# Sorting the late queue of a backward kernel by chunk: chunk 0's operations unpinned, chunk 1's put off by one iteration

## The chip, the core and the metric

The kernel runs on one core of a Trainium2 chip. The metric is the device time of one execution in microseconds (us); lower is better. A core has five engines that run side by side and meet through semaphores: TensorE (PE, matmuls), VectorE (DVE), ScalarE (ACT), GpSimd (POOL) and SyncE (SP, which here only issues DMAs). Each engine takes its instructions in a fixed order.

## The reference: what is computed

Forward pass and all gradients of a speech joint network. Two convolutions over time (3 taps, each followed by gelu and by taking every second step) reduce 16000 steps to 4000; the result is projected, combined with 8 label vectors by tanh, and projected again.

```python
def _fwd_reference(x, w1, w2, g, w_f, w_g, w_o):
    ...
    xp = jnp.pad(x, ((0,0),(pad,pad),(0,0)))
    h = jnp.zeros_like(x)
    for i in range(K):
        h = h + jnp.einsum("btc,cd->btd", xp[:, i:i+T, :], w1[i])
    h = _gelu(h)[:, ::2, :]
    ...
    f = _gelu(f)[:, ::2, :]
    fe = jnp.einsum("btd,de->bte", f, w_f)
    ge = jnp.einsum("bud,de->bue", g, w_g)
    j = jnp.tanh(fe[:, :, None, :] + ge[:, None, :, :])
    return jnp.einsum("btud,dv->btuv", j, w_o)

def reference(x, w1, w2, g, w_f, w_g, w_o, grad_out):
    ...
    _out, _vjp = jax.vjp(_f, x, w1, w2, g, w_f, w_g, w_o)
    _grads = _vjp(grad_out)
```

x is 2 x 16000 x 256 in bf16, the output 2 x 4000 x 8 x 256. For each gelu the kernel needs its value in the forward pass and its derivative in the backward pass.

## The kernel before

The 4000 steps of each of the two batches are cut into 8 chunks of 512 (CW, the last one 416): 16 chunks, numbered n. A loop over n (line 783) does in iteration n: the joint part of chunk n (tanh, output, gradients, in four steps "up" of two labels u each), the backward convolutions of chunk n - 1, and the forward convolutions of chunk n + 1. The forward part of chunk 0 is done ahead of the loop (the prologue, line 777), so iteration 0 has the forward part of chunk 1 and no backward part.

The units of work are Python generators. `weave` (line 702) steps through the joint part (`joint_units`) and takes, by a ratio, units of a `fill` chain, which holds the convolutions. After each joint unit it calls `pump`, which emits operations of two queues: `later`, the first half of a gelu (its value), and, when that is empty, `lazy`, the second half (its derivative).

`gelu` (line 202) makes both halves. The first has a square on ACT (g_sq), a step on DVE (line 214, g_s), a sigmoid on ACT (g_s again) and a product on DVE, which gives HT or FT. The second has five DVE operations on the same scratch tiles: two tensor_scalar and three tensor_tensor, which give the derivative G1 or G2. All the emitted calls of the first half stand at line 198 or 291 in the profile, those of the second at line 200. A chunk has three gelus (even and odd steps of the first convolution, and the second convolution), so 15 operations of 128 x 1024; chunk 0 does each in two halves of 128 x 512, so 30. The scratch tiles come from a pool of three buffers per name (`gel3`); chunk 0 takes tiles of `rows` (pool `rowp`, six) instead. With a chunk's second halves two small copies on POOL go into the queue: G1h, the last column of G1 kept for the next chunk, and G, that column's place in the next chunk.

A scheduler decides the order of the instructions on each engine when the program is built. What is wrapped in `tc.keep_in_program_order` ("pinned") stays where the program emits it; other instructions may be moved ahead or back, as their data allow. In the kernel before, `pump` pins every operation of `lazy`:

```python
            elif lazy and lazy_on[0]:
                tc.keep_in_program_order(lazy.popleft()())
```

`lazy_on` is set when the second convolution of the next chunk has been emitted (line 295), and cleared at the end of each iteration, after the whole queue has been emptied (lines 832 and 833). The flag is first set in the prologue, by chunk 0. So in iteration 0 the 30 operations of chunk 0 and the 15 of chunk 1 are all emitted; in a later iteration n, the 15 of chunk n + 1. They are first read in iteration n + 2: G2 by line 354 (GF), G1 by line 385 (GH).

Other lines that matter: 249 (first convolution, PE) and 252 (its eviction, ACT, g_x); 283 and 286 (second convolution, the same); 306 and 308 (FE, the projection); 316 (tanh, JT); 540 (JSQ, the square of JT, ACT); 546 (gradient of JT, PE, with weights WOT and the loaded GOT) and 548 (its product with 1 - JT squared, DVE, NGZ); 567 (sum of NGZ over u, POOL, ACCN); 396 and 398 (JT transposed on PE and copied to JR by DVE in iteration 0; later iterations do it with a DMA, line 580); 644 and 646 (output block, PE, and its eviction OUT, ACT); 693 (gradient of w_o, PE, GWO_ps); 333 and 335 (the other weight gradients' accumulation, DVE, ACC). PSUM has seven tiles for all of these results ("ps" and "pst", pool `psp`).

Of the kernel before, what the change touches and what calls it, by code (L numbers as in the profile page):

```python
# [28 lines left out]
CW = 512  # L29
# [4 lines left out]
def kernel(  # L34
# [22 lines left out]
    nc = tc.nc  # L57
# [7 lines left out]
    def geom(n):  # L65
        b, ci = chunks[n]
        c0 = ci * CW
        return b, ci, c0, min(CW, MQ - c0)
# [33 lines left out]
    def ps_f32():  # L102
        return psp.tile([P, 512], FP32, name="ps", tag="ps")
# [24 lines left out]
    S = [dict() for _ in range(G)]  # L128
# [61 lines left out]


    later, lazy = deque(), deque()
    lazy_on = [False]

    def pump(k):
        for _ in range(k):
            if later:
                later.popleft()()  # L198
            elif lazy and lazy_on[0]:
                tc.keep_in_program_order(lazy.popleft()())  # L200

    def gelu(xb, W, h, gp, off, kts=((0, KT),), spare=False, pinned=False):

        pin = tc.keep_in_program_order if pinned else (lambda ins: ins)
        sq, s = scratch("g_sq", spare), scratch("g_s", spare)
        TT, TS, STT = nc.vector.tensor_tensor, nc.vector.tensor_scalar, nc.vector.scalar_tensor_tensor
        first, second = [], []
        for (k0, k1) in kts:
            sq_, s_, x_ = sq[:, k0:k1, :W], s[:, k0:k1, :W], xb[:, k0:k1, :W]
            h_, gp_ = h[:, k0:k1, off:off + W], gp[:, k0:k1, off:off + W]  # L210
            first += [
                partial(nc.scalar.activation, out=sq_, in_=x_, func=ACT.Square, scale=ROOT_K),
                lambda s_=s_, sq_=sq_, x_=x_: pin(
                    STT(out=s_, in0=sq_, scalar=1.0, in1=x_, op0=ALU.add, op1=ALU.mult)),  # L214
                partial(nc.scalar.activation, out=s_, in_=s_, func=ACT.Sigmoid, scale=GELU_A),
                partial(TT, out=h_, in0=s_, in1=x_, op=ALU.mult),
            ]
            second += [
                partial(TS, out=sq_, in0=sq_, scalar1=3.0 * GELU_A, scalar2=GELU_A, op0=ALU.mult, op1=ALU.add),
                partial(TS, out=gp_, in0=s_, scalar1=-1.0, scalar2=1.0, op0=ALU.mult, op1=ALU.add),  # L220
                partial(TT, out=sq_, in0=sq_, in1=gp_, op=ALU.mult),
                partial(TT, out=sq_, in0=sq_, in1=h_, op=ALU.mult),
                partial(TT, out=gp_, in0=sq_, in1=s_, op=ALU.add),
            ]
        return first, second
# [4 lines left out]
    def conv_units(n):  # L230
        b, ci, c0, W = geom(n)
        seconds = []
        st = S[n]
        HT = htp.tile([P, 2, KT, CW + 2], BF16, name="HT")
        G1 = g1p.tile([P, 2, KT, CW + 2], BF16, name="G1")
        st["HT"], st["G1"] = HT, G1
        if ci == 0:
            nc.gpsimd.memset(HT[:, 1, :, 1:2], 0.0)
        else:
            nc.gpsimd.tensor_copy(out=HT[:, 1, :, 1:2], in_=S[n - 1]["HT"][:, 1, :, CW + 1:CW + 2])  # L240
        taps = {0: ((1, 0, 0), (2, 1, 0), (0, 3, -1)), 1: ((0, 1, 0), (2, 3, 0), (1, 2, 0))}
        for par in range(2):
            xb = gel.tile([P, KT, CW], BF16, name="g_x")
            for mt in range(KT):
                ps = ps_f32()
                k = 0
                for (i, c, sh) in taps[par]:
                    for kt in range(KT):
                        nc.tensor.matmul(ps[:, :W], lhsT=W1[:, i, kt, mt * P:(mt + 1) * P],  # L249
                                         rhs=st["X", c][:, kt, 16 + sh:16 + sh + W], start=(k == 0), stop=(k == 5))  # L250
                        k += 1
                nc.scalar.copy(out=xb[:, mt, :W], in_=ps[:, :W])
                yield
            first, second = gelu(xb, W, HT[:, par], G1[:, par], 2, HALVES if n == 0 else ((0, KT),), n == 0,
                                 pinned=n > 1 and par == 1)
            later.extend(first)
            seconds += second
            if n == 0:
                pump(len(first))
        lazy.extend(seconds)  # L260
        if ci > 0:
            lazy.append(lambda: nc.gpsimd.tensor_copy(out=G1[:, :, :, 1:2], in_=S[n - 1]["G1h"][:]))
        if ci < NCH - 1:
            st["G1h"] = halo.tile([P, 2, KT, 1], BF16, name="G1h")
            lazy.append(
                lambda: nc.gpsimd.tensor_copy(out=st["G1h"][:], in_=G1[:, :, :, CW + 1:CW + 2]))

    def conv2_units(n):
        b, ci, c0, W = geom(n)
        st = S[n]  # L270
        HT = st["HT"]
        if n > 0:
            pump(len(later))
        FT = ftp.tile([P, KT, CW], BF16, name="FT")
        G2 = ftp.tile([P, KT, CW], BF16, name="G2")
        st["FT"], st["G2"] = FT, G2
        xb = gel.tile([P, KT, CW], BF16, name="g_x")
        for mt in range(KT):
            ps = ps_f32()
            k = 0  # L280
            for (i, par, off) in ((1, 0, 2), (0, 1, 1), (2, 1, 2)):
                for kt in range(KT):
                    nc.tensor.matmul(ps[:, :W], lhsT=W2[:, i, kt, mt * P:(mt + 1) * P],  # L283
                                     rhs=HT[:, par, kt, off:off + W], start=(k == 0), stop=(k == 5))
                    k += 1
            nc.scalar.copy(out=xb[:, mt, :W], in_=ps[:, :W])
            yield
        first, second = gelu(xb, W, FT, G2, 0, HALVES if n == 0 else ((0, KT),), n == 0)
        if n == 0:
            for f in first:  # L290
                f()
        else:
            later.extend(first)
        lazy.extend(second)
        lazy_on[0] = True

    def fe_units(n):
        b, ci, c0, W = geom(n)
# [484 lines left out]
    for n in range(G):  # L783
        back, fwd = n > 0, n + 1 < G
        conv = conv_units(n + 1) if fwd else iter(())
        parts = []
        if back:
            for (o, M) in blocks(window(n - 1)[1] - window(n - 1)[0]):
                load_x5(n - 1, o, M)
            d1, e, gwf = d1_units(n - 1), e_units(n - 1), gwf_units(n - 1)  # L790
            nfn = (len(blocks(geom(n - 1)[3])) + 1) // 2
            d5, gw2 = d5_units(n - 1), gw2_units(n - 1)
            nhg = KQ
            parts += [islice(conv, 2), islice(d1, 1), islice(conv, 1), d1, islice(conv, 1),
                      islice(gwf, 1), islice(d5, 1), conv, islice(gwf, nfn - 1), islice(d5, 1), islice(gw2, 1),
                      islice(d5, 1), islice(gw2, 1), d5, islice(gw2, nhg - 2), gwf, gw2]
        else:
            parts += [conv, iter([None] * 3)]
        conv2 = conv2_units(n + 1) if fwd else iter(())
        if back:  # L800
            parts += [islice(e, 1), islice(conv2, 1), islice(e, 1), conv2, islice(e, 5)]
        else:
            parts.append(conv2)
            parts.append(iter([None] * 3))
        if fwd:
            parts.append(fe_units(n + 1))
        if back:
            parts.append(e)
        fill = chain(*parts)
        ratio = (0.85 if n > 0 else 0.28) if n + 1 < G else 0.72  # L810
        for up in range(U // 2):
            step = n * (U // 2) + up
            if n + 2 < G:
                load_x(n + 2, (1, 0, 3, 2)[up])
            if step + 1 < len(orderp):
                load_go(*orderp[step + 1])
            for i in range(2):
                if 2 * step + 4 + i < len(order):
                    load_got(*order[2 * step + 4 + i])

            def ahead():
                for i in range(2):
                    if 2 * step + 2 + i < len(order):
                        tanh(*order[2 * step + 2 + i])
                if step + 1 < len(orderp):
                    load_jr(*orderp[step + 1])

            weave(joint_units(n, up, ahead), fill, ratio)
            if up == U // 2 - 1:
                for _ in fill:  # L830
                    pump(2)
                pump(len(later) + len(lazy))
                lazy_on[0] = False
    def small_gradients():
        t_ = gel.tile([P, 512], BF16, name="g_x", tag="g_x")
        nc.scalar.copy(out=t_[:], in_=GWO_ps[:].rearrange("p k v -> p (k v)"))
# [32 lines left out]
    n = G - 1  # L869
# [35 lines left out]
```

## Time and profile before

| | us |
|---|---|
| median of 3 runs | 854.25 (853.19 to 855.17) |
| the profiled execution | 852.57, its span 850.8 |
| PE busy | 821.0 (96%) |
| ACT busy | 680.5 (80%) |
| DVE busy | 628.5 (74%) |
| POOL busy | 392.1 (46%) |

The mean granted TensorE clock of the profiled execution is 0.992. The costliest groups of instructions of the DVE and POOL are these (line, engine, operation, out<-in, shapes, count; busy us, mean ns of one; idle time before them and what ended most of it):

```profile
L567 POOL TENSOR_TENSOR ACCN<-ACCN,NGZ 128x1024 f32<-128x1024 f32 (+1 forms) x80 | 168.4, 2104 | 126.2 <-DVE NGZ L548 124.2
...
L548 DVE SCALAR_TENSOR_TENSOR NGZ<-JSQ,ps 128x512 bf16<-128x512 bf16 (+1 forms) x256 | 166.0, 668 | 26.9 <-PE ps L546 21.6
...
L214 DVE SCALAR_TENSOR_TENSOR g_s<-g_sq,g_x 128x1024 bf16<-128x1024 bf16 (+1 forms) x45 | 58.1, 1291 | 67.9 <-ACT g_sq L198 67.5
```

A stage is read with the busy time of each engine in a stretch of the span; a wait of an engine is put down to the instruction that released it.

### The profile page before, as it was taken

What the parts mean: (1) busy time and instruction counts of PE and PEld (TensorE: products, weight loads), DVE (VectorE), ACT (ScalarE), POOL (GpSimd) and SP (SyncE); (2) the same over time, 40 slices, a digit from 0 to 9 for tenths busy, and PEclk for the clock granted to TensorE, in tenths of its full rate; (3) what the DMA queues carried; (4) which work ended last, traced back from release to release, by engine and by line L of the source; (5) the groups of instructions that cost most, each with busy time, mean ns of one, the idle gap of its engine ahead of it and who ended that gap; (6) DMA issues with size and microseconds to landing.
All of it is one profiled execution on the core that took longest, in us unless ns stands there. A gap on an engine that the chain in (4) does not pass through costs nothing.

```text
span 850.8 us, 17235 instructions
## 1 busy us (share of the span) xinstructions
PE 821.0 (96%) x6478; PEld 600.5 (71%) x6552; DVE 628.5 (74%) x1190; ACT 680.5 (80%) x1064; POOL 392.1 (46%) x452
## 2 busy tenths in 40 slices
PE   8877999999999999999999999999999999999998
PEld 4444776777767677787767678677777767777876
DVE  4599777687877868777776887767797776868552
ACT  4786989697997969798796969969797896979533
POOL 1144454454444445454554644444553544545650
PEclk9998999999999999999999999999999999999999
DMA  9976999999999999999999999999999999998942
GB/s 187 188 156 148 232 234 187 227 238 203 238 259 215 239 233 235 247 213 243 205 261 210 247 218 244 172 223 267 219 252 204 247 285 201 251 242 193 226 146 90
DMA packets 379280, 185.60 MB, mean 218 GB/s; under 512 B 326786, under 2 KB 362907, under 8 KB 379198
## 3 DMA queue, kind: packets, MB, share of 16 engines
q1 hardware_dynamic: 359550, 115.19, 75.9%
q0 software_dynamic: 19648, 69.32, 26.0%
q8 instruction: 51, 0.84, 0.4%
q14 instruction: 31, 0.25, 0.1%
HBM read 54.43 MB, written 50.34 MB: 123 GB/s over the span
## 4 chain that ended last, share of the span: by engine, by line
PE 56%; ACT 21%; DVE 16%; issue 4%; DMA 2%; POOL 0%; SPq 0%; DVEq 0%; ACTq 0%; POOLq 0%
PE ps L644 8%; PE GWO_ps L693 7%; PE ps L546 7%; ACT JT L316 7%; PE ps L495 7%; PE ps L518 6%; PE ps L454 5%; DVE NGZ L548 5%; PE ps L283 4%; PE pst L396 4%; ACT OUT L646 3%; PE ps L249 3%; ACT JSQ L540 3%; DVE G L200 3%; DVE HT L198 3%
## 5 line engine op out<-in xcount | busy, mean ns | idle before, releaser
L567 POOL TENSOR_TENSOR ACCN<-ACCN,NGZ 128x1024 f32<-128x1024 f32 (+1 forms) x80 | 168.4, 2104 | 126.2 <-DVE NGZ L548 124.2
L540 ACT ACTIVATE JSQ<-JT 128x1024 bf16<-128x1024 bf16 (+1 forms) x128 | 133.2, 1046 | 73.4 <-DVE NGZ L548 72.4
L548 DVE SCALAR_TENSOR_TENSOR NGZ<-JSQ,ps 128x512 bf16<-128x512 bf16 (+1 forms) x256 | 166.0, 668 | 26.9 <-PE ps L546 21.6
L316 ACT ACTIVATE JT<-FE,GE 128x512 bf16<-128x512 f32 (+1 forms) x256 | 170.2, 721 | 0.5
L646 ACT CAST OUT<-ps 128x512 bf16<-128x512 f32 x248 | 145.4, 599 | 16.8 <-PE ps L644 16.7
L644 PE MATMUL ps<-WO,JT 128*128 128x256 bf16 x992 | 149.3, 275 | 9.1 <-DVE NGZ L548 6.2
L546 PE MATMUL ps<-GOT,WOT 128*128 128x512 bf16 (+1 forms) x472 | 135.6, 376 | 5.7 <-DVE JR L398 3.0
L693 PE MATMUL GWO_ps<-GO,JR 128*128 128x256 bf16 x992 | 140.8, 275 | 0.0
L644 PEld LDWEIGHTS <-JT 128*128 128x128 bf16 x992 | 96.0, 98 | 37.9 <-issue 11.0
L693 PEld LDWEIGHTS <-JR 128*128 128x128 bf16 x992 | 95.9, 99 | 18.9 <-issue 1.6
L214 DVE SCALAR_TENSOR_TENSOR g_s<-g_sq,g_x 128x1024 bf16<-128x1024 bf16 (+1 forms) x45 | 58.1, 1291 | 67.9 <-ACT g_sq L198 67.5
L673 POOL DMA_DIRECT2D out_dram<-OUT x64 | 49.6, 774 | 119.1 <-ACT OUT L646 117.2
L495 PE MATMUL ps<-W1T,GH 128*128 128x256 bf16 (+2 forms) x768 | 104.2, 273 | 0.0
L498 ACT CAST GX<-ps 128x512 bf16<-128x512 f32 (+2 forms) x128 | 74.8, 584 | 23.8 <-PE ps L495 19.1
L249 PE MATMUL ps<-XC,W 128*128 128x512 bf16 (+1 forms) x370 | 88.9, 375 | 3.8 <-DMA XC<-in_x_dram 3.4
L518 PE MATMUL ps<-rows,X 128*128 128x256 bf16 (+2 forms) x768 | 92.3, 273 | 0.0
L495 PEld LDWEIGHTS <-GH 128*128 128x128 bf16 (+2 forms) x768 | 75.0, 99 | 12.4 <-issue 0.8
L518 PEld LDWEIGHTS <-X 128*128 128x128 bf16 (+2 forms) x768 | 74.6, 98 | 12.9 <-issue 1.3
L546 PEld LDWEIGHTS <-WOT 128*128 128x128 bf16 x512 | 49.0, 98 | 45.8 <-issue 5.7
L335 DVE TENSOR_TENSOR ACC<-ACC,ps 128x512 f32<-128x512 f32 x84 | 57.3, 682 | 28.8 <-PE ps L454 24.2
L249 PEld LDWEIGHTS <-W 128*128 128x128 bf16 x384 | 37.7, 98 | 41.2 <-issue 4.5
L508 POOL DMA_DIRECT2D out_dram<-GX x60 | 33.7, 561 | 71.9 <-ACT GX L498 67.9
(138 smaller groups left out, 1309.0 us busy)
## 6 DMA issues: line engine op xcount, KB each, us to landing
GO<-in_grad_out_dram SPq DMA_DIRECT2D x56, 512.0 KB, 5.2
out_dram<-OUT POOLq DMA_DIRECT2D x56, 512.0 KB, 5.8
X<-in_x_dram POOLq DMA_DIRECT2D x58, 320.0 KB, 8.6
out_dram<-GX POOLq DMA_DIRECT2D x55, 256.0 KB, 4.9
GO<-in_grad_out_dram SPq DMA_DIRECT2D x8, 384.0 KB, 3.8
out_dram<-OUT POOLq DMA_DIRECT2D x8, 384.0 KB, 4.8
JR<-JT SPq DMA_TRANSPOSE x136, 5.9
GOT<-in_grad_out_dram SPq DMA_TRANSPOSE x128, 5.2
```

The costliest lines, as they stand in the source:

```text
L249: nc.tensor.matmul(ps[:, :W], lhsT=W1[:, i, kt, mt * P:(mt + 1) * P], rhs=st["X", c][:, kt, 16 + sh:16 + sh + W], start=(k == 0), stop=(k ...
L316: nc.scalar.activation(out=JT[:, mt, :W], in_=S[n]["FE"][:, mt, :W], func=ACT.Tanh, bias=GE[:, b, mt, u:u + 1], scale=1.0)
L495: nc.tensor.matmul(ps[:Mx, cj * D:(cj + 1) * D], lhsT=GH[:, par, kt, j:j + Mx], rhs=W1T[:, i, kt, :], start=(k == 0), stop=(k == last))
L498: nc.scalar.copy(out=t[:Mx, 2 * cp:2 * cp + 2, :], in_=ps[:Mx, :])
L518: nc.tensor.matmul(ps[:, dt * D:(dt + 1) * D], lhsT=st["X5", o][:M, i + 2 * par, dt * P:(dt + 1) * P], rhs=t[:M, j + 2 * par:j + 2 * par + ...
L540: nc.scalar.activation(out=JSQ[:, :, :W], in_=JT[:, :, :W], func=ACT.Square)
L546: nc.tensor.matmul(ps[:, :W], lhsT=WOT[:, kt, mt * P:(mt + 1) * P], rhs=GOT[:, kt, :W], start=(kt == 0), stop=(kt == KT - 1))
L548: nc.vector.scalar_tensor_tensor(out=NGZ[:, mt, :W], in0=JSQ[:, mt, :W], scalar=1.0, in1=ps[:, :W], op0=ALU.subtract, op1=ALU.mult, accum_ ...
L567: nc.gpsimd.tensor_tensor(out=out, in0=in0, in1=st["NGZ", u][:, :, :W], op=ALU.add)
L644: nc.tensor.matmul(ps[:M, j * V:(j + 1) * V], lhsT=st["JT", u][:, kt, o:o + M], rhs=WO[:, kt, :], start=(kt == 0), stop=(kt == KT - 1))
L646: nc.scalar.copy(out=OUT[:M, k, :], in_=ps[:M, :])
L693: nc.tensor.matmul(GWO_ps[:, dt, :], lhsT=JR[:M, j, dt, k, :], rhs=GO[:M, k, j * V:(j + 1) * V], start=(n_gwo[0] == 0), stop=(n_gwo[0] == ...
```

## The change

The queue holds pairs of a chunk number and an operation, and the flag becomes the highest chunk whose operations may be emitted (`lazy_to`). Three things follow. Chunk 0's operations are emitted as before in iteration 0, but not pinned, so the scheduler may move them. In iteration 0 the second convolution of chunk 1 does not raise `lazy_to` (n is 1), so chunk 1's 15 operations and its two POOL copies stay in the queue until iteration 1, where they are emitted from its start, pinned. From chunk 2 on, operations are emitted as before. No operation is added or removed.

```diff
-    lazy_on = [False]
+    lazy_to = [-1]
 
     def pump(k):
+
         for _ in range(k):
             if later:
                 later.popleft()()
-            elif lazy and lazy_on[0]:
-                tc.keep_in_program_order(lazy.popleft()())
+            elif lazy and lazy[0][0] <= lazy_to[0]:
+                n, op = lazy.popleft()
+                ins = op()
+                if n > 0:
+                    tc.keep_in_program_order(ins)
+
+    def put_off(n, ops):
+        lazy.extend((n, op) for op in ops)
...
-        lazy.extend(seconds)
+        put_off(n, seconds)
         if ci > 0:
-            lazy.append(lambda: nc.gpsimd.tensor_copy(out=G1[:, :, :, 1:2], in_=S[n - 1]["G1h"][:]))
+            put_off(n, [lambda: nc.gpsimd.tensor_copy(out=G1[:, :, :, 1:2], in_=S[n - 1]["G1h"][:])])
         if ci < NCH - 1:
             st["G1h"] = halo.tile([P, 2, KT, 1], BF16, name="G1h")
-            lazy.append(
-                lambda: nc.gpsimd.tensor_copy(out=st["G1h"][:], in_=G1[:, :, :, CW + 1:CW + 2]))
+            put_off(n, [lambda: nc.gpsimd.tensor_copy(out=st["G1h"][:], in_=G1[:, :, :, CW + 1:CW + 2])])
...
-        lazy.extend(second)
-        lazy_on[0] = True
+        put_off(n, second)
+        if n != 1:
+            lazy_to[0] = n
...
                 pump(len(later) + len(lazy))
-                lazy_on[0] = False
+                lazy_to[0] = max(lazy_to[0], n + 1)
```

## The prediction, made before the changed kernel was run

> **What bounds the kernel now.** I read first the 40 slices of the page, then the busy time by stage, then who PE waited for, then the timelines of the four engines between 20 and 110 us.
>
> ```profile
> PE   8877999999999999999999999999999999999998
> ...
> DVE  4599777687877868777776887767797776868552
> ```
>
> A slice is 21.3 us. From slice 5 on PE is at nine tenths and nothing off PE can win anything. Only slices 1 to 4 have room, and there DVE is full in slices 3 and 4. The stages (columns: stretch and length; busy us and instructions of PE, PEld, DVE, ACT, POOL; granted clock, DMA share, GB/s):
>
> ```profile
> 32.00:85.30 53.30, 41.30 (x260) 25.40 (x263) 51.44 (x106) 39.03 (x60) 22.80 (x20) 0.87 0.70 151
> 85.30:108.30 23.00, 22.84 (x189) 16.51 (x191) 16.79 (x33) 22.10 (x33) 10.26 (x10) 1.00 1.12 239
> 135.90:158.90 23.00, 22.58 (x187) 16.29 (x189) 17.16 (x30) 17.60 (x26) 9.27 (x10) 1.00 1.19 191
> ```
>
> The first is iteration 0 of the loop (n = 0): DVE is busy 51.44 of 53.30 us, PE idles 12.0. The second is the first half of iteration 1, the third the same half of iteration 2: PE is full in both. Whom PE waited for in iteration 0 (us in total, times, longest):
>
> ```profile
> PE ps L644 <- DVE NGZ L548: 6.2, 4, 2.5
> PE ps L249 <- DMA XC<-in_x_dram: 3.4, 1, 3.4
> PE ps L546 <- DVE JR L398: 3.0, 2, 2.1
> PE ps L306 <- DVE FT L198: 1.1, 1, 1.1
> PE pst L396 <- DVE JR L398: 0.9, 2, 0.7
> ```
>
> All but the load wait is DVE: PE has no free PSUM tile (7 of "ps"), because DVE evicts too late. What DVE does instead is the late queue, line 200 (same columns, DVE alone):
>
> ```profile
> 32.00:85.30 53.30, 28.96 (x45) 0.87 0.70 151
> ```
>
> 45 operations, 28.96 of the 51.44 us. How one of them delays PE and ACT (start, duration, engine, in brackets the idle time before):
>
> ```profile
> 47.03 0.42 DVE L200 TENSOR_TENSOR G<-rows 128x512 bf16<-128x512 bf16 x1
> 47.37 2.22 DVE L200 TENSOR_SCALAR rows<-rows 128x512 bf16<-128x512 bf16 x1
> 49.50 0.67 DVE L548 SCALAR_TENSOR_TENSOR NGZ<-JSQ,ps 128x512 bf16<-128x512 bf16 x1
> ...
> 47.27 2.16 POOL L567 TENSOR_TENSOR ACCN<-ACCN,NGZ 128x1024 f32<-128x1024 f32 x1 [4.00 <-DVE NGZ L548]
> ...
> 50.24 1.86 PE L644 MATMUL ps<-WO,JT 128*128 128x256 bf16 x8 [2.48 <-DVE NGZ L548]
> ...
> 70.15 1.06 ACT L198 ACTIVATE g_s<-g_s 128x1024 bf16<-128x1024 bf16 x1 [4.25 <-DVE g_s L214]
> ```
>
> The same TENSOR_SCALAR takes 0.28 elsewhere; started just after a POOL add it takes 2.22, to the add's end. The eviction behind it is 2 us late, PE idles 2.48 us. After such a gap the granted clock is low: 0.66 in 49 to 54, 0.67 in 65 to 70, 0.62 in 76 to 80, so 1.7 + 1.65 + 1.5 = 4.9 us more are lost.
>
> **The change, part by part.** By the compiled order no instruction is added or lost on any engine; only places differ, on DVE from its first scalar_tensor_tensor (12 us) to the second ACC copy of iteration 1 (104 us), on PE from 43 us up to the second conv of iteration 1 (82 us). Everything behind is in the old order.
>
> 1. Chunk 0's 30 operations (6 groups of 5) go ahead. Unpinned, all stand before the first JR copy (32.67 us), 17 of them behind the last FT. Start to start they cost 0.21 (TENSOR_SCALAR) or 0.34 us (TENSOR_TENSOR): 6 x (2 x 0.21 + 3 x 0.34) = 8.6 us. DVE has the room: idle from 24.66 to 32.67, and POOL is idle then. Those put ahead of FT delay it by about 0.9 us (four before the first g_s of FT, 1.2 us against 0.93 idle; three each ahead of the next two); the 17 behind take 5 us, to about 30.7, two before the JR copy. The cover is this wait:
>
> ```profile
> 27.36 1.03 PE L249 MATMUL ps<-XC,W 128*128 128x512 bf16 x4
> 31.81 0.59 PE L249 MATMUL ps<-XC,W 128*128 128x512 bf16 x2 [3.42 <-DMA XC<-in_x_dram]
> ```
>
> PE stands still for a load until 31.81, and JSQ, done at 30.8, has 1 us left. Cost 0; without the cover 0.9.
>
> 2. Chunk 1's 15 operations leave iteration 0. With both parts DVE has 51.44 - 28.96 = 22.5 us of work there, and no longer sets the pace. ACT is next. Its idle time from 37 to 85 us is 0.23 + 1.08 + 0.27 + 1.71 + 0.23 + 4.25 + 1.41 + 1.74 + 0.15 = 11.1 us. I walked the new order of ACT on from 49.2 with the old durations: g_s of the odd half (old 54.43) runs at 49.2, FE (old 72.61) at 63.2, the first eviction of iteration 1 (old 85.54) at 74.2: 11.3 us, nearly all of ACT's idle time; PE's work of some 28 us fits in. One wait should remain: the g_s step on DVE before FT comes while POOL adds (g_sq ready at 59.0, add from 58.8 to 61.0) and FT's chain loses 1.8 us. So 11.1 - 1.8 = 9.3 us. Bounds: 11.1, all of ACT's idle time; and 4.4, if only ACT's waits for g_s (6.2 us in this stretch) go, less 1.8. I take 9.3, near the upper end, as every named wait but the load is DVE's.
>
> 3. Iteration 1 gets the 15 operations, in its first half: 3 x (2 x 0.34 + 3 x 0.60) = 7.4 us, on 16.79 of 23.0 busy: 24.2, over by 1.2. Some will meet POOL, whose adds fill 8.10 us there; in the same half of iteration 2, an HT multiply takes 2.31 for 0.69. My walk through the new order from the first NGZ (82.89) brings the third GH product 1.7 us late, the fourth 3 to 5, the ACC copies 2 to 4. PSUM is tight just there: in every iteration PE waits 0.3 us for GH. Part of the lateness ends in the idle 0.37 + 2.92 us DVE has before 112.6. I take 3.0 us; bounds 0 (all in slack) and 1.2 + 8.1 = 9.3 (each add blocks DVE for its whole length).
>
> 4. Waits that move. In POOL's queue the G1h copy of chunk 1 now waits in iteration 1 for the odd half's last G; behind it stand an add, two halo copies and an output store. The copies are 0.2 to 0.6 us, the store's buffer is wanted 12 us later: 0. On SP one GOT load passes one JR transpose: 0, since DMA is least loaded there (0.21 to 0.44 between 54 and 80).
>
> Sum: -9.3 + 3.0 = -6.3 us. The profiled execution took 852.57 (span 850.8), 1.7 below the median of 854.25; so 846.3 for it and **848.0** for the median.
>
> **Rivals.**
> *Larger gain.* Iteration 1 hides the operations (its ACT, not DVE, is full at 22.10 of 23) and the 1.8 us do not occur: -11.1, 843.1. For it: PE's idle time plus low clock is 16.9 us, more than ACT's. Against it: DVE has no room for 7.4 us there. The Trainium skill, "TensorE: Matmul & The Clock Gate", Part 1, lets the clock halve after an idle window of about 3.4 us; this trace shows 0.66 after a gap of 2.48. By the page the 4.9 us would not belong to the gaps, PE would win at most its 12.0 us idle, still above ACT's 11.1.
>
> *No change.* The queue is only moved: iteration 0 gains near its lower bound, 4.4, since ACT's own order delays PE, and iteration 1 gives 4 back: 853.9. For it: ACT is 100% busy from 85.3 to 100 already. Against it: ACT's gaps in iteration 0 are DVE's.
>
> *Slower.* The POOL adds of iteration 1 block DVE at nearly each of the four: 9.3 us late, PSUM runs out, PE stands over 2 us and its clock drops for another 1.7: loss 11.0. With a gain of 9.3 that is +1.7, 855.95; with 4.4, 860.9. It decides once PE idles over 9 us between 75 and 100. For it: the row of 2.22 for 0.28. Against it: NGZ and the products that read PSUM are not delayed (all 20 NGZ of iteration 0 take 0.67 to 0.68), and an operation started ahead of the add runs free. The Trainium skill, "SBUF — State Buffer", SBUF: two separate sides, speaks for it: DVE operations with two SBUF inputs or in a two-port mode and a GpSimd operation lock each other out for a whole instruction. The rows agree (2.22 ends with the add).
>
> *It does not do what it says.* Chunk 0's operations could delay FT and so everything: +0.9 at most, by part 1.
>
> **How the numbers follow.** Forecast (3 to 9 us won) 0.62, larger gain 0.22, no change 0.09, slower 0.07 (the delayed FT in it). A measurement here can tell 0.2%, 1.7 us. Faster: 0.62 + 0.22 and a little of the third, 0.86; same 0.08; slower 0.06. The range starts at 843.0 (all of 11.1) and ends at 851.5 (4.4 won, 1.7 given back); above lie the last two cases.
>
> **What would show it.** Right: no line-200 operation on DVE between 32 and 75; PE's waits for NGZ and JR in iteration 0 under 3 us, the clock there near 1.0 after 37; the first tanh of chunk 1 about 9 us earlier; then PE idle of 1 to 5 us between 75 and 98 with releaser GH, NGZ or ACC, and a lag that stays constant from 110 on. Wrong: PE's waits go over to ACT in iteration 0 (step 2), the clock is low in iteration 1 (step 3), or PE's wait for the load moves from 31.81 (step 1).

## The result

| | before | after |
|---|---|---|
| median of 6 runs, us | 853.72 (852.12 to 858.67) | 841.15 (840.20 to 845.39) |
| profiled execution, us | 852.57 | 840.20 |
| its span, us | 850.8 | 838.4 |
| mean granted clock | 0.992 | 1.000 |

The changed kernel takes 0.9855 of the time, 95% interval 0.9823 to 0.9888: 12.6 us less. The forecast was 848.0, 6.3 less. The direction was right, the gain is twice as large, and the time lies 1.9 us below the range. The ratios and their intervals, here and below, leave out executions more than 1.5% above the fastest of their kernel; medians and ranges hold them.

The 40 slices of the changed kernel's page (busy tenths; the last line is the granted clock):

```profile
PE   8889999999999999999999999999999999999998
...
DVE  5778888776778778687877769777688776869552
...
PEclk9999999999999999999999999999999999999999
```

DVE's full slices 3 and 4 are gone (9 9 became 7 8), and PE is at nine tenths from slice 4 on, one earlier. Line numbers from 207 on are 7 higher than before (6 in the second convolution); the late queue is now line 202. First the stages, cut for both kernels at the same marks on PE's timeline: the first output block, and the first GF matmul of each iteration. The three windows of before are iterations 0, 1 and 2 (columns: stretch and length; busy us and instructions of PE, PEld, DVE, ACT, POOL; granted clock, DMA share, GB/s):

```profile
36.80:84.05 47.25, 35.64 (x225) 21.67 (x227) 46.06 (x89) 35.96 (x55) 22.45 (x20) 0.89 0.70 151
84.05:134.29 50.24, 49.98 (x399) 37.08 (x403) 38.67 (x75) 46.98 (x73) 24.37 (x27) 1.00 1.09 230
134.29:184.92 50.63, 50.11 (x398) 36.96 (x402) 39.02 (x70) 42.88 (x67) 23.84 (x27) 1.00 1.13 213
```

The same three of after:

```profile
33.99:68.39 34.40, 31.36 (x226) 20.28 (x228) 21.24 (x50) 32.92 (x51) 19.82 (x14) 1.00 0.94 207
68.39:120.82 52.43, 50.92 (x398) 37.13 (x402) 47.81 (x89) 47.37 (x75) 27.49 (x30) 1.00 1.09 228
120.82:172.50 51.68, 50.49 (x398) 37.01 (x402) 39.45 (x72) 43.82 (x68) 24.85 (x29) 1.00 1.13 226
```

Iteration 0 went from 47.25 to 34.40 us: 12.85 won. In it PE's idle time fell from 47.25 - 35.64 = 11.61 to 3.04 us (8.57 won), and its busy time from 35.64 to 31.36 (4.28 won), since the clock went from 0.89 to 1.00. DVE, 97% busy there before, is 62% busy now; ACT has taken its place with 32.92 of 34.40. Iterations 1 and 2 give back 2.19 and 1.05. The first convolution starts 0.96 us earlier, and the stretch from there to the loop is 1.85 shorter. Together 0.96 + 1.85 + 12.85 - 2.19 - 1.05 = 12.4, the difference of the spans.

What PE still waits for in iteration 0 of after (us in total, times, longest):

```profile
PE ps L289 <- DVE JR L405: 1.2, 1, 1.2
PE ps L313 <- DVE FT L199: 0.9, 1, 0.9
PE ps L289 <- DVE HT L199: 0.3, 1, 0.3
PE pst L403 <- DVE NGZ L555: 0.2, 1, 0.2
PE pst L403 <- DVE JR L405: 0.2, 1, 0.2
```

The four waits for NGZ (6.2 us) are gone, and of 11.0 us of waits for DVE in this stage 2.8 are left. The late operations of after, line 202 alone (stretch and length, DVE busy and count, clock, DMA):

```profile
11.00:34.00 23.00, 9.24 (x30) 1.00 1.02 203
34.00:68.40 34.40, 0.23 (x1) 1.00 0.94 207
68.40:94.00 25.60, 11.18 (x15) 1.00 1.11 225
```

Chunk 0's 30 stand ahead of the loop and take 9.24 us. Chunk 1's 15 stand in iteration 1 (the one in the second row is the first of them; it starts at 68.17) and take 0.23 + 11.18 = 11.4, where undisturbed ones of 0.42 (TENSOR_SCALAR) and 0.68 us (TENSOR_TENSOR) would take 3 x (2 x 0.42 + 3 x 0.68) = 8.6. One operation of after in that stretch:

```profile
87.75 1.75 DVE L202 TENSOR_SCALAR G<-g_s 128x1024 bf16<-128x1024 bf16 x1
```

It takes 1.75 us, against 0.42 for the same operation at 116.92.

### The profile page after: what moved, and what is told of

Read it like the earlier page. It is cut to its first block, busy times and chain, and to the rows that moved or that the text cites. A ratio compares the mean times of both kernels' runs of the same rounds, so it can differ in the third digit from the quotient of the medians.

```text
span 838.4 us, 17233 instructions
## 1 busy us (share of the span) xinstructions
PE 816.8 (97%) x6478; PEld 598.3 (71%) x6552; DVE 620.0 (74%) x1190; ACT 679.3 (81%) x1064; POOL 395.0 (47%) x452
## 4 chain that ended last, share of the span: by engine, by line
PE 59%; ACT 20%; DVE 14%; issue 4%; DMA 3%; POOL 0%; DVEq 0%; ACTq 0%; POOLq 0%
PE GWO_ps L700 8%; PE ps L651 8%; PE ps L502 7%; PE ps L553 7%; ACT JT L323 7%; PE ps L525 6%; PE ps L461 5%; PE ps L289 5%; PE pst L403 4%; DVE NGZ L555 4%; PE ps L256 4%; ACT OUT L653 3%; DVE G L202 3%; ACT JSQ L547 3%; DVE HT L199 3%
## 5 line engine op out<-in xcount | busy, mean ns | idle before, releaser
L502 PEld LDWEIGHTS <-GH 128*128 128x128 bf16 (+2 forms) x768 | 75.1, 99 | 12.4 <-issue 0.8
```

Of the source, the lines that this page charges most:

```text
L502: nc.tensor.matmul(ps[:Mx, cj * D:(cj + 1) * D], lhsT=GH[:, par, kt, j:j + Mx], rhs=W1T[:, i, kt, :], start=(k == 0), stop=(k == last))
```

## The experiments

All stage times below are cut at the marks used above, with iteration 0 cut once more at chunk 1's first FE matmul: "to FE" is set by chunk 0's late operations or their absence, "FE to GF" by chunk 1's. "Ahead" is from the first convolution to the first output block. Medians stand with their lowest and highest run. The columns are worked out from each kernel's PE timeline, in one profiled execution each; how far such numbers vary between executions of one kernel is shown further down.

```
us           ahead  to FE  FE-GF  iter 0  iter 1  iter 2
before       27.24  35.18  12.07   47.25   50.2    50.6
after        25.39  25.95   8.45   34.40   52.4    51.7
chunk 0 only 25.45  25.95  14.38   40.33   54.4    50.6
chunk 1 only 26.09  34.29   9.12   43.41   52.2    51.7
before+idle  24.00  33.75  12.15   45.90   50.2    50.6
after, 3 ops 24.90  25.94   8.46   34.40   51.3    50.6
both unpinned26.88  28.34   9.48   37.82   50.3    50.6
FT undelayed 25.54  26.35   8.45   34.80   52.4    51.7
after+idle   24.46  24.50   8.46   32.96   52.4    51.7
none pinned  25.31  28.35   7.82   36.17   51.8    52.0
5 ops early  24.47  25.03   8.45   33.48   53.9    50.6
10 ops early 24.46  26.79   7.82   34.61   51.7    50.6
before-5 adds24.95  29.72  10.71   40.43   52.0    50.6
```

### Each half of the change alone

Chunk 0's operations unpinned, chunk 1's left in iteration 0 (against after):

```diff
-        if n != 1:
-            lazy_to[0] = n
+        lazy_to[0] = n
```

> The changed kernel with chunk 1's 15 operations emitted in iteration 0 again, pinned, as before; only chunk 0's are unpinned. In the profile before, the 45 late operations took 28.96 us of DVE in iteration 0: chunk 1's 14.1, chunk 0's 14.9. Theory A (each part frees DVE for itself, gains add): about half of the 12.6 us, 846 to 848, with line 202 on DVE between 60 and 82 us and a low clock there once or twice. Theory B (DVE is only just over its limit, one part is enough): 841 to 843. Theory C (it matters only that chunk 1 leaves the end of iteration 0): 851 to 854.

Chunk 1's put off, chunk 0's pinned in iteration 0 as before (against after):

```diff
-                if n > 0:
-                    tc.keep_in_program_order(ins)
+                tc.keep_in_program_order(ins)
```

> The changed kernel with chunk 0's operations pinned in iteration 0 as before; only chunk 1's are put off. Theory A: the other half, 846 to 848; chunk 0's operations fill DVE from 33 to about 60 us, the half clock after the wait for the load at 31.8 stays. Theory B: 841 to 843. Theory C (chunk 1 alone matters): 841 to 843 too, then told apart from B by the other run.

Measured: chunk 0 alone 848.60 (847.04 to 860.38), ratio 0.9912 [0.9878, 0.9946]; chunk 1 alone 853.01 (850.45 to 857.17), ratio 0.9965 [0.9931, 1.0]. By the ratios the two bring some 7.5 and 3.0 us, and the whole 12.6; neither brings all of it, and the intervals are too wide (4.6 to 10.4, and 0 to 5.9) to say whether the two add up. Chunk 1 alone lies outside the ranges of all three of its theories, chunk 0 alone just above that of its theory A. The stages say more: up to FE the chunk-0 half brings 9.2 us, exactly what the whole change brings, and the chunk-1 half 0.9; from FE to GF the chunk-1 half brings 2.95 of 3.6, and the chunk-0 half loses 2.3. What DVE does there with only chunk 0's moved (its timeline: start, duration, operation):

```profile
64.35 2.35 DVE L202 TENSOR_SCALAR g_sq<-g_sq 128x1024 bf16<-128x1024 bf16 x1
66.62 0.67 DVE L554 SCALAR_TENSOR_TENSOR NGZ<-JSQ,ps 128x512 bf16<-128x512 bf16 x1
...
69.38 2.27 DVE L202 TENSOR_TENSOR G<-g_sq,g_s 128x1024 bf16<-128x1024 bf16 x1
```

And POOL in the same kernel at the same time:

```profile
63.98 2.44 POOL L573 TENSOR_TENSOR ACCN<-ACCN,NGZ 128x1024 f32<-128x1024 f32 x1 [4.48 <-DVE NGZ L554]
68.66 2.44 POOL L573 TENSOR_TENSOR NGFE<-ACCN,NGZ 128x1024 bf16<-128x1024 f32 x1 [2.24 <-DVE NGZ L554]
```

Chunk 1's pinned operations start just behind a POOL add and end about with it, an NGZ stands behind them, and the picture that the prediction shows at 47 us appears here at 64: from FE to GF this kernel takes 5.9 us more than the changed one, and in iteration 1 another 2.0. So each half clears its own half of iteration 0, and chunk 0's alone passes part of the load on.

### Chunk 1's operations in iteration 1, and the clock ahead of the loop

Against after, 12 of chunk 1's 15 operations are left out:

```diff
-        put_off(n, seconds)
+        put_off(n, [op for i, op in enumerate(seconds) if n != 1 or i % 5 == 4])
...
-        put_off(n, second)
+        put_off(n, [op for i, op in enumerate(second) if n != 1 or i % 5 == 4])
```

> The changed kernel with 12 of chunk 1's 15 late operations left out (only the last of each five is done, so the gradients that pass through chunk 1 are wrong). It measures what the moved operations cost in iteration 1. By the traces PE's lead falls from 15.7 us at 74 to 13.5 at 96, 2.2 us. If the moved operations cause that, the time falls by 1.5 to 2.5 us against the changed kernel, to about 839. If the lead is lost because iteration 1 is bound by ACT anyway, it falls by less than 0.7.

Measured: 839.45 (837.26 to 849.95), ratio 0.9791 [0.9734, 0.9847]. Iterations 1 and 2 take 51.3 + 50.6, 2.2 us less than in the changed kernel, as forecast; that is the price of the 12 operations, the whole loss of iteration 2 among it. Against the first before profile 1.1 us stays in iteration 1 without them. The profiled execution took 849.95, for another reason (PE's waits late in the loop):

```profile
PE GWO_ps L700 <- DMA JR<-JT: 9.8, 4, 4.3
```

The other edit fills PE's wait for the load ahead of the loop with 12 matmuls whose results nobody reads (against before, behind the prologue's chain; the helper `warm` is the kernel's own):

```diff
+    for _ in warm(12):
+        pass
```

> The kernel before, with 12 matmuls of the idle tile (their result is not used) put on PE ahead of the loop, so that PE's gap before the load's end (3.42 us in the profile before, 2.28 after) is filled. If the drop of the granted clock to 0.66 between 32 and 37 us comes from that gap and cost the 1.5 to 2 us that the changed kernel won before its loop, the time falls by 1 to 2 us against the kernel before and the clock in 32 to 37 is near 1.0. If these 2.8 us were only an earlier start of that one execution, the time stays within 0.5 us.

Measured: 850.30 (847.87 to 856.46), ratio 0.9944 [0.9908, 0.9981]. "Ahead" falls to 24.00, the lowest of all, and iteration 0 to 45.90. Filling this gap helps, by some 4.8 us (1.6 to 7.9), more than either expectation, and the clock between 32 and 37 us is 1.00. But the gap isn't what the change removes: 11.5 of iteration 0's 12.85 us are still to be had in this kernel.

### Is the put-off needed, is the pin, and does FT's delay count

Chunk 0 and chunk 1 both unpinned, neither put off (against after):

```diff
-                if n > 0:
+                if n > 1:
...
-        if n != 1:
-            lazy_to[0] = n
+        lazy_to[0] = n
```

> Nothing is put off: chunk 1's operations are emitted in iteration 0 again, but unpinned like chunk 0's; by the compiled order the scheduler spreads them over iteration 0, from behind the first HT on. In the trace after, DVE idles about 14 us between 32 and 68 us, room for the 7.4 us of chunk 1. Theory 1 (what counts is that no late operation stands in front of an eviction that PE waits for): about as fast as the changed kernel, or up to 3 us faster, since iterations 1 and 2 do not lose the 3.2 us; 838 to 841. Theory 2 (the operations must leave iteration 0): as with chunk 0 alone unpinned, 847 to 849.

Measured: 843.05 (841.15 to 847.76), ratio 0.9891 [0.9838, 0.9943]. Iterations 0 to 2 take 37.82 + 50.3 + 50.6 = 138.7 us, the changed kernel's 34.40 + 52.4 + 51.7 = 138.5. The median lies 2 us above the range of theory 1 and 4 below that of theory 2; the stages speak for theory 1. Chunk 1's operations stay in iteration 0 and iterations 1 and 2 lose nothing; the price is in iteration 0, where some stand ahead of FT, one of them 2.56 us long, for 0.68, behind a POOL add (PE's waits):

```profile
PE ps L312 <- DVE FT L199: 3.0, 1, 3.0
```

So operations of the late queue don't have to leave iteration 0; they must not stand in front of what PE waits for.

No pin at all, no put-off (against after):

```diff
-                if n > 0:
-                    tc.keep_in_program_order(ins)
+                pass
...
-        if n != 1:
-            lazy_to[0] = n
+        lazy_to[0] = n
```

> Nothing is put off and no late operation is pinned in any iteration. If pinning is what makes the late operations block evictions in iteration 0 only, the later iterations, where PE is 99% busy, stay at 50.6 us each, and the time is that of the run with both chunks unpinned, 838 to 841. If pinning protects the later iterations, each of 14 loses, and 1 us each would give 852 to 855.

Measured: 856.18 (854.09 to 863.54), ratio 1.0042 [1.0002, 1.0082]. Iteration 0 is still 11 us shorter than before, but a steady iteration takes 52.0 instead of 50.6 us. In PE's waits behind the first iterations stand small waits, once in most iterations, which neither before nor after has:

```profile
PE ps L551 <- DVE ACC L340: 3.4, 10, 0.3
PE ps L288 <- DVE ACC L340: 2.6, 9, 0.3
```

They make up 6.0 of some 13 us that the iterations from 3 on lose; what the rest is stays open. The run with both chunks unpinned differs from this one only in the pin from chunk 2 on, and its iteration 2 takes 50.6. So the pin costs in iteration 0 and pays in the others.

All pinned, but chunk 0's 30 emitted at the end of the prologue's chain, behind FT (against after):

```diff
-                if n > 0:
-                    tc.keep_in_program_order(ins)
+                tc.keep_in_program_order(ins)
...
+    pump(len(lazy))
```

> The changed kernel, but chunk 0's 30 operations are emitted and pinned right behind the prologue, so all stand behind the last FT, 13 of them among the first evictions of the loop. FT is not delayed by 0.9 us, so PE reaches the wait for the load earlier and its gap is longer, as before (over 3 us). If that gap decides the clock at the loop's start, the granted clock in 32 to 37 us falls to about 0.66 and the time is 1 to 2 us over the changed kernel's, plus up to 2 for the 13 operations: 842 to 845. If the gap does not decide it: within 1 us of 841, clock near 1.0 there.

Measured: 840.59 (839.77 to 844.42), ratio 0.9863 [0.9816, 0.991]. FT is not delayed, PE's wait for the load is

```profile
PE ps L255 <- DMA XC<-in_x_dram: 2.9, 1, 2.9
```

and "ahead" is within 0.15 us of the changed kernel's. The clock between 32 and 37 us is 1.00 all the same, so a gap of 2.9 us doesn't decide it. That "ahead" is so close may be chance, as it varies by over 1 us between executions of one kernel; but PE waits for the load in both kernels. So FT's delay costs nothing here, as long as the load is late; and the place in the program, with no freedom for the scheduler, does the same as the unpinning.

### How much of the loss was POOL

Against before, five of the seven POOL adds of chunk 0 are left out (line 567; its condition):

```diff
-        if u == 0:
+        if u == 0 or (n == 0 and 1 < u < U - 1):
```

> The kernel before with 5 of the 7 POOL adds of chunk 0 left out (labels 2 to 6 are not summed, so gradients through chunk 0 are wrong). In the profile before the 45 late operations take 28.96 us in iteration 0 where undisturbed ones would take 19.6 (30 of mean 0.36, 15 of mean 0.58), so 9.3 us are spent behind POOL adds. If this blocking is a main part of the loss, iteration 0 (47.2 us) falls by 4 to 8 us. If the number of operations alone fills DVE, it falls by less than 2.

Measured: 845.77 (844.10 to 853.57), ratio 0.9893 [0.9837, 0.9948]. All 45 late operations are in iteration 0 as before, but take

```profile
32.00:85.30 53.30, 22.22 (x45) 0.97 1.00 186
```

22.22 us instead of 28.96 (line 200 alone, DVE), and iteration 0 falls by 6.8, from 47.25 to 40.43 us. So about half of what the change wins there was DVE standing still behind POOL's adds, 5.5 of 9.2 up to FE and 1.4 of 3.6 behind it; that the rest falls to the operations' own work in front of the evictions is a subtraction that no run tests, and two of the seven adds are still there. The Trainium skill, "SBUF — State Buffer", SBUF: two separate sides, says that a GpSimd operation and DVE operations in a two-port mode or with two SBUF inputs lock each other out for a whole instruction; this run agrees, with 6.7 us less DVE time for five adds of some 2.1 us.

### Versions beyond the changed kernel

After with 8 idle matmuls behind the prologue's chain (`+    for _ in warm(8):` / `+        pass`):

> The changed kernel with 8 matmuls of the idle tile ahead of the loop, as in the run of the kernel before with 12 (which was about 4 to 5 us faster than the kernel before in its fast runs, and 5.4 us ahead in the trace from iteration 1 on). If the filled gap saves mostly the low clock, which the changed kernel does not have there, little is left: 0 to 1.4 us faster (the rest of the load wait), 839.5 to 841. If the two gains add, 836 to 837.

Measured: 838.65 (837.72 to 854.76), ratio 0.9827 [0.9779, 0.9876]; ahead 24.46 and iteration 0 32.96, and the span is 835.9 against 838.4. The median lies between the two forecast ranges. As that of after comes from another set of runs, and the two intervals overlap, the times don't separate the two kernels.

The same, with 5 or 10 of chunk 1's operations, those of its first convolution, left in iteration 0 unpinned, and the rest in iteration 1 (for the 10):

```diff
+        if n == 1:
+            put_off(0, seconds[:10])
+            seconds = seconds[10:]
```

> The changed kernel with the 8 idle-tile matmuls ahead of the loop, and with the first 5 of chunk 1's 15 operations (even half) emitted in iteration 0, unpinned; 10 stay in iteration 1. Theory (DVE has idle time in iteration 0 and is over its limit in the first half of iteration 1; what is moved back costs nothing there if it does not stand before FT): iterations 1 and 2 lose about 2 instead of 3.2 us, and the time is 1 us under the run with the 8 matmuls alone (838.65), about 837.5. Rival (the loss of iteration 1 comes from ACT's backlog, or the 5 operations delay FT): no gain, 838.5 to 840.

> The same with 10 of the 15 (both halves of the first convolution) in iteration 0, 5 in iteration 1. Theory: iterations 1 and 2 lose about 1 us, 836.5 to 838, if the 10 do not delay FT. Rival: as with all 15 unpinned, where FT stood behind them and PE waited 3.0 us for FT: 839 to 841.

The changed kernel itself, beside them on the same chip:

> The changed kernel once more, beside the others on one chip. If the 2.8 us that its first profile won ahead of the loop belong to the change, the new profile shows 25.4 us from the first conv to the first output block and a clock of 1.0 from 32 to 37; if they are chance, 26 to 27 us and a low clock there are as likely. Time 840 to 843.

Measured: 5 early 843.02 (839.99 to 857.52), ratio 0.9827 [0.9773, 0.9881]; 10 early 839.34 (837.23 to 840.23), ratio 0.9788 [0.974, 0.9837]; the changed kernel 842.93 (840.91 to 845.06), ratio 0.9833 [0.9788, 0.9878]. The 5 are inconclusive, above both ranges: in the profiled execution, the longest of the six, iteration 1 took 53.9 us and iteration 2 50.6, and PE lost 12.4 us to late transposing DMAs (last section). With the 10, all six runs lie below all of the changed kernel's: this version beats both kernels. Its profile has iterations 0 to 2 at 136.9 us (changed kernel 138.5) and 0.6 to 0.9 us less ahead. Which of its two edits brings how much of the 3.6 us between the medians isn't settled by times, as the idle matmuls alone ran in another set. By the stages the 10 bring next to nothing on top: ahead and iterations 0 to 2 add up to 161.4 us with them and to 161.5 with the idle matmuls alone, since what iterations 1 and 2 win is lost in iteration 0, where PE waits 1.6 us for FT instead of 0.5. That is what the rival said, and the time lies in its range.

### What differs between executions of one kernel

Before three times more and after once more, unchanged, one execution each:

> The kernel before, unchanged, for another profile. If the low clock at the loop's start (0.66 between 32 and 37 us) and the 27.2 us from the first conv to the first output block belong to the pinned late operations, all profiles of this kernel show them; the changed kernel showed 25.4 and 25.1 us and a clock of 1.0 in two of two. If it is chance, some show about 25.5 us and a full clock.

> A third profile of the kernel before: 27 us and a low clock at the loop's start if they belong to it, about 25.5 us and a full clock possible if by chance.

> A fourth profile of the kernel before: 27 us and a low clock at the loop's start if they belong to it, about 25.5 us and a full clock possible if by chance.

> The changed kernel, a third profile: if its start is free of the low clock by its order of work, 25.0 to 25.5 us again; if by chance, 26 to 27 is possible.

In the table "start" is the start of the first convolution, and the first row of each kernel is the profile shown so far:

```
us           start  ahead  iter 0  iter 1  iter 2  time
before        9.56  27.24   47.25   50.2    50.6   852.57
before        8.64  26.67   47.69   52.0    50.6   853.71
before        9.06  26.36   47.29   52.0    50.6   855.01
before        8.65  25.45   48.29   52.0    50.6   852.10
after         8.60  25.39   34.40   52.4    51.7   840.20
after         9.42  25.07   34.41   52.4    51.7   840.91
after         8.82  26.49   34.41   52.4    51.7   840.83
```

Three things follow. "Ahead" varies by 1.8 us in the kernel before and by 1.4 in the changed one, and the clock at the loop's start varies in both: between 32 and 37 us it is 0.66, 0.85, 0.80 and 1.00 in the four, and 1.00, 1.00 and 0.81 in the three. So the low clock there doesn't belong to one of the kernels, and most of the 2.8 us of the first pair up to the loop is chance (0.8 with the means below). Iteration 0 is 47.25 to 48.29 in one and 34.40 to 34.41 in the other. And the first before profile had the shortest iteration 1 of four; in the others PE waits there once for an NGZ (PE's waits between 85 and 135 us in the second before profile):

```profile
PE pst L396 <- DVE NGZ L548: 1.6, 1, 1.6
```

With means of the four and the three: prologue and start 35.4 against 34.6, iteration 0 47.6 against 34.4, iterations 1 and 2 102.15 against 104.1. That is 0.8 + 13.2 - 1.95 = 12.05 us, of the 12.6 between the medians.

## Why the prediction was right in direction and half the size

**Step 2, iteration 0: forecast -9.3, measured -12.85 (13.2 against four before profiles).** This is the mis-sized term, and its upper bound (11.1, "all of ACT's idle time") was no bound. Between the marks ACT's idle time fell from 47.25 - 35.96 = 11.29 to 34.40 - 32.92 = 1.48 us: 9.8, close to the 9.3. What failed is the cap by ACT: its work between the marks fell as well, from 35.96 to 32.92 us, and 9.8 + 3.0 = 12.85. Of the four instructions fewer, two tanh and an eviction now come after PE's second mark, and one tanh comes ahead of the first. The walk along ACT itself was nearly right. The first output eviction of iteration 1, before and after:

```profile
85.54 0.57 ACT L646 CAST OUT<-ps 128x512 bf16<-128x512 f32 x1
```

```profile
71.70 0.61 ACT L653 CAST OUT<-ps 128x512 bf16<-128x512 f32 x1
```

Counted from the first output block it comes 48.74 - 37.71 = 11.0 us earlier; the walk gave 11.3, before the 1.8 came off. But PE's GF stands 1.49 us ahead of this eviction in before and 3.31 in after: PE won another 1.8 us by running further ahead of ACT. So the idle time of an engine that follows PE doesn't bound what PE wins in a stage, where PE can run ahead of it. The 1.8 us taken off for FT's chain, that was to lose them behind a POOL add, were too much, and make up the other half of the 3.55 us missing (its step on DVE in after):

```profile
56.50 1.57 DVE L221 SCALAR_TENSOR_TENSOR g_s<-g_sq,g_x 128x1024 bf16<-128x1024 bf16 x1 [1.45 <-ACT g_sq L199]
```

It takes 1.57 us, 0.35 more than the 1.22 of an undisturbed one; the rest of ACT's last 1.48 us of idle time has other causes. PE's own rows were in the prediction as an argument for the larger gain (16.9 us of idle time and low clock); 12.85 of them came.

**The wait moved with the eviction, as forecast.** PE's waits for NGZ and JR in iteration 0 fell to 1.6 us ("under 3"), the clock of this profile is 1.00 in the whole stage, and no late operation stands between 34 and 68. The first tanh of chunk 1 starts at 61.55 instead of 73.23, counted from the first output block 8.9 us earlier ("about 9"). The two experiments on the halves and the one on the adds show the cause: chunk 0's operations set the first half, chunk 1's the second, and about half of the whole is DVE blocked behind POOL.

**Step 3, iteration 1: forecast +3.0, measured +3.2 in the two first profiles and +1.95 against all four.** The size is right to about 1 us, and so is the walk along DVE: counted from the NGZ at which the walk starts (82.89, in after 67.56) the third GH product comes 2.1 us late, the fourth 4.0, the ACC copies 3.8 to 4.1. What the operations lose to POOL is 11.4 - 8.6 = 2.8 us of DVE's time. What was wrong is whom PE would wait for. For GH it waits nothing in iteration 1, and 0.5 us in iteration 2 where before has 0.3 (nor is that wait in every iteration of before: it has none in iteration 1). Its longest wait in iteration 1 of after is one for ACT:

```profile
PE ps L651 <- ACT rows L405: 0.7, 1, 0.7
```

Behind it stand only 0.3 us for an ACC copy and 0.2 for an output eviction of ACT. So part of the lead over ACT that PE won in iteration 0 may be given back here; no run shows how much. That iteration 2 loses 1.05 was not foreseen; with 12 operations left out it is back at 50.6, so the loss is theirs. The 1.1 us that stay in iteration 1 of that run lie inside what before itself varies (50.2 and 52.0), and what they are is open.

**Step 1, chunk 0's operations ahead: forecast 0, right.** The cover held: FT is delayed, and PE waits for the load all the same (PE's timeline of after, in brackets its idle time):

```profile
30.48 0.59 PE L256 MATMUL ps<-XC,W 128*128 128x512 bf16 x2 [2.28 <-DMA XC<-in_x_dram]
```

The kernel with FT undelayed waits for the load as well. The 30 operations keep DVE busy for 9.24 us; 8.6 had been worked out from start to start. The 2.8 us by which the first pair of profiles differ up to the loop were nobody's forecast, and the repeats show prologues as far apart in one kernel.

**Step 4, POOL's and SP's queues: forecast 0.** Neither queue's moved instructions show up as a releaser of PE's waits in iterations 0 to 2 of after, so nothing contradicts it. The DMA share that it gives (0.21 to 0.44 between 54 and 80) leaves out the stretch from 65 to 70, where it is 0.86; nothing hung on it.

**The sum.** Of the 6.1 us missing between the spans, 3.55 are step 2, 2.8 the start and prologue of the first pair, and -0.2 step 3. **The rivals:** "larger gain" came nearest and was half right: the 1.8 us hardly occurred (0.35), but iteration 1 doesn't hide the operations, and ACT's idle time was its cap too. "No change" and "slower" let iteration 1 give back 4 and 9.3 us; by the run without 12 of the operations it is 2.2, iteration 2 included.

## What to carry to other kernels

Where an engine that evicts PSUM also works off deferred operations in a fixed order, look at each stage by itself: a pin that protects the steady iterations (50.6 against 52.0 us) may put the deferred work in front of the evictions in a stage that has fewer matmuls to hide it (47.3 against 34.4). Work that must run there belongs in an earlier stretch where its engine idles anyway, or behind what PE waits for, and leaving the stage altogether is not needed. When such a gain is sized, take PE's idle time and its low-clock stretches between two marks as the most it can be (16.9 us here, of which 12.85 came), and don't cap it by the idle time of an engine downstream.

## What was not expected of the hardware

**The clock after short gaps.** It falls in some executions and not in others, after gaps of the same kind. The window behind the load wait, in two executions of the same kernel before (second, then fourth; columns as in the stages):

```profile
32.00:37.00 5.00, 4.91 (x36) 3.36 (x35) 4.89 (x15) 2.99 (x6) 0.79 (x1) 0.85 0.58 122
```

```profile
32.00:37.00 5.00, 5.00 (x40) 3.37 (x38) 5.00 (x14) 3.63 (x8) 1.66 (x1) 1.00 0.58 120
```

The first had 0.85 there behind a gap of 3.17 us, the other 1.00, and its gap was 3.00:

```profile
30.48 0.59 PE L249 MATMUL ps<-XC,W 128*128 128x512 bf16 x2 [3.00 <-DMA XC<-in_x_dram]
```

The gap of 2.48 us of the prediction was followed by 0.66. The Trainium skill, "TensorE: Matmul & The Clock Gate", Part 1, lets the clock halve after an idle window of about 3.4 us; here a gap of 2.48 us had a low clock behind it and one of 3.00 had not. What decides it is open; the length of one gap alone does not.

**Transposing DMAs that land late.** In some profiled executions PE waits, late in the loop, for the DMA that transposes JT into JR: 2.5 us in the third of the kernel before (855.01 us) and nothing in its other three (852.10 to 853.71), 0.6 us in the changed kernel's first, 9.8 us in four waits in the one shown above, 12.4 us in the kernel with 5 early. No edit here touches these DMAs; the DMA share stands at 1.0 to 1.2 from iteration 1 on, and why they land late is open.
